# First head pair of block-sparse attention loaded in fp32 by hardware queues, mask rows spread by DMA, late transposes moved to the DMA crossbar

## The chip, the cores and the metric

The kernel runs on one core of one Trainium2 chip. The metric is device time in microseconds (us), from the median of a few executions. The kernel before takes 288.36 us (three runs, 288.26 to 288.44). TensorE is called PE in the profile, VectorE DVE, ScalarE ACT, GpSimd POOL and SyncE SP.

## The reference, cut to what matters

Attention with a block mask (band, global rows and columns, three sampled blocks for each block row), then an MLP-Mixer on its output: token mixing, residual, channel mixing, residual.

```python
# q, k, v: (4, 8, 768, 64) fp32; mask blocks of 32; 24 x 3 sampled blocks, int64
scores = scale * np.matmul(q, k.transpose(0, 1, 3, 2))
scores = np.where(mask, scores, -1000000000.0)
attn = np.exp(scores - scores.max(-1, keepdims=True)); attn = attn / (attn.sum(-1, keepdims=True) + 1e-09)
x = np.matmul(attn, v)             # regrouped to (4, 768, 512)
h = np.maximum(x.transpose(0, 2, 1) @ w_tok1, 0.0) @ w_tok2     # 768 -> 256 -> 768
u = x + h.transpose(0, 2, 1)
out = u + np.maximum(u @ w_ch1, 0.0) @ w_ch2                    # 512 -> 1536 -> 512
```

## The kernel before

The 32 heads are taken in 16 pairs. A pair has 12 steps: two query halves of 384 by six key chunks of 128. Each step is a pair of score matmuls (QK, one for each head), one exponential of 128x768 on ScalarE, and six matmuls with V (PV). The mask costs no instruction in a step. K and Q get 24 more rows each: on K's side a pattern that says which key belongs to which block, on Q's side 0 or -30000 for each block. The QK matmul then contracts over 88 rows instead of 64.

A small planner in the Python program simulates the engines with fixed costs and decides from that the order in which each engine gets its instructions. A changed cost or dependency can therefore move instructions far away. On TensorE the planner fills free time during attention with token and channel matmuls of batches that are through.

```python
# loads: cast from fp32 to bf16 on POOL's software queue, pair by pair
nc.gpsimd.dma_start(out=raw[:, :, :, :], in_=APx(src, 2 * p * S * D, ...))        # L230
# mask on 24 partitions R, after the sample has landed
nc.vector.tensor_copy(out=sampf[R, :], in_=samp64[R, :].bitcast(I32))
for dst, col in ((allow, 0), (eq0, 2), (eq1, 4)):
    nc.vector.tensor_scalar(..., op0=ALU.is_equal)
for other in (eq0, eq1, bandg):
    nc.vector.tensor_tensor(..., op=ALU.max)
nc.vector.tensor_scalar(out=t2add[R, :], ..., op0=ALU.mult, op1=ALU.add)
# mask rows: a matmul, two ScalarE copies, then 15 VectorE copies for eight head buffers
nc.vector.tensor_copy(out=bufs[n][R, :], in_=indf if nm == "k" else qtb[0][R, :])  # L356
# each pair: relayout on VectorE, 6 + 6 TensorE transposes, 4 evacuations (VectorE or ScalarE)
nc.vector.tensor_copy(out=buf[0:64, :], in_=i)                                     # L439
# ... step: QK (L470), exponential (L478), PV (L520)
# ... u: 24 TensorE transposes per batch (L628), first channel matmul L664, second L686
```

The softmax here doesn't subtract the row's maximum and nothing guards it: scores larger than these inputs give would overflow.

## Time and profile before

| what | before |
|---|---|
| span of the profiled run | 287.1 us |
| first QK matmul starts | 10.92 us |
| first exponential starts | 12.03 us |
| 25th exponential starts | 34.99 us |
| last exponential ends | 160.91 us |
| last QK matmul ends | 159.98 us |
| from there to the last matmul's end | 123.1 us |
| from there to the end of the span | 4.1 us |

These are boundaries between stages, and they add up to the span: attention ends with the last QK, and the tail is the PE work that is left then. The timelines give the first five, the windows the last three. The lines themselves stand in the prediction below.

Two rows of the chain of waits of the kernel before are added here, because the prediction did not look at them. Columns: start, duration, what.

```profile
13.73 0.64 PE ps L470 x2
14.38 0.33 PE po L520 x6
```

Two QK matmuls take 0.64 us here and six PV matmuls 0.33 us. The prediction works with 0.163 us for one QK and 0.030 us for one PV, the pace of later stages, which would make 0.33 and 0.18. TensorE runs at half of its later pace at this point. The first four exponentials take 16.88 - 12.03 = 4.85 us there instead of 4 x 0.750 = 3.0, so 1.85 of the 2.6 us of waits that the prediction puts down to VectorE fell before the stretch of the chain that it read, which starts at 16.9.

### The profile page before, as it was taken

The page shows a single profiled execution, that of the slowest core. Times are in us where ns is not written, and L with a number is a line of the kernel's source. Part 1 is how long each engine was busy: PE and PEld are TensorE (multiplying, and loading weights), DVE is VectorE, ACT ScalarE, POOL GpSimd, SP SyncE. Part 2 cuts the span into 40 slices and gives each one's busy share as a digit, 9 for nine tenths or more (in the row PEclk, how much of TensorE's full clock was granted, in tenths as well). Part 3 has the DMA queues.
Part 4 walks back from the last instruction along what each step waited for, and adds up shares of the span by engine and source line. Part 5 has one row for each costly group of instructions (what it writes and reads, how often), then busy time and mean ns, then how long its engine had stood idle before and what let it go on. Part 6 is the DMA issues. An engine that isn't in the chain of part 4 may idle for free.

```text
span 287.1 us, 6351 instructions
## 1 busy us (share of the span) xinstructions
PE 269.9 (94%) x2682; PEld 175.5 (61%) x2690; DVE 130.2 (45%) x286; ACT 191.9 (67%) x286; POOL 45.0 (16%) x70
## 2 busy tenths in 40 slices
PE   0799899999999999999999999999999999999994
PEld 0366676678777777777777754456544654456441
DVE  5789966557777569765546341210022001200121
ACT  1589999999999999999999642037501770067200
POOL 7956554522211000000000000000000000000000
PEclk9999999999999999999999999999999999999999
DMA  4999999996254100000000001220022001210122
GB/s 55 134 204 202 214 201 205 201 185 87 39 73 66 23 2 2 0 2 3 2 0 2 2 0 39 106 76 0 2 110 84 29 0 73 94 54 0 38 102 82
DMA packets 19168, 20.07 MB, mean 70 GB/s; under 512 B 1348, under 2 KB 15428, under 8 KB 19140
## 3 DMA queue, kind: packets, MB, share of 16 engines
q0 software_dynamic: 15648, 13.37, 30.3%
q1 hardware_dynamic: 3492, 6.29, 5.8%
q8 instruction: 21, 0.34, 0.5%
q14 instruction: 7, 0.06, 0.1%
HBM read 26.74 MB, written 6.29 MB: 115 GB/s over the span
## 4 chain that ended last, share of the span: by engine, by line
PE 73%; ACT 14%; DVE 6%; issue 2%; DMA 2%; POOL 2%; POOLq 0%; DVEq 0%; ACTq 0%
PE pm_ch L686 22%; PE pm_ch L664 21%; ACT et L478 14%; PE ps L470 14%; PE po L520 8%; PE pm_tok L578 3%; PE pm_tok L603 2%; DMA kraw<-in_k_dram 2%; DVE qtb L439 1%; PE pm_ut L628 1%; PE tq L421 1%; DVE ktb L439 1%; PE tk L421 1%; DVE x L535 1%; DVE klay L394 1%
## 5 line engine op out<-in xcount | busy, mean ns | idle before, releaser
L478 ACT ACTIVATE et<-ps 128x768 bf16<-128x768 f32 x192 | 143.2, 810 | 4.2 <-PE ps L470 3.2
L470 PE MATMUL ps<-qtb,ktb 88*128 88x384 bf16 x384 | 95.3, 329 | 4.0 <-ACT et L478 1.7
L560 ACT ACTIVATE rc<-pm_ch 128x384 bf16<-128x384 f32 x84 | 41.2, 491 | 60.7 <-PE pm_ch L664 44.8
L520 PEld LDWEIGHTS <-et 128*128 128x128 bf16 x1152 | 56.0, 97 | 22.8 <-DVE x L535 1.9
L664 PE MATMUL pm_ch<-uT,w_ch 128*128 128x384 bf16 x384 | 68.6, 326 | 0.2 <-DVE rc L562 0.2
L686 PE MATMUL pm_ch<-w_ch,rc 128*128 128x512 bf16 x280 | 62.4, 379 | 0.4
L520 PE MATMUL po<-vaug,et 128*128 128x65 bf16 x1152 | 61.5, 193 | 0.5 <-ACT et L478 0.2
L694 DVE TENSOR_TENSOR o<-pm_ch,x 128x512 f32<-128x512 f32 x24 | 16.6, 692 | 98.7 <-PE pm_ch L686 98.7
L664 PEld LDWEIGHTS <-w_ch 128*128 128x128 bf16 x384 | 37.0, 98 | 23.1 <-issue 0.3
L686 PEld LDWEIGHTS <-rc 128*128 128x128 bf16 x288 | 28.2, 98 | 33.6
L470 PEld LDWEIGHTS <-ktb 88*128 88x128 bf16 x384 | 34.2, 99 | 11.9 <-issue 4.4
L439 DVE COPY ktb<-tk 64x768 bf16<-64x768 bf16 x29 | 16.0, 552 | 17.5 <-PE tk L421 17.2
L611 DVE TENSOR_TENSOR x<-pm_tok,x 128x512 bf16<-128x512 f32 x24 | 16.2, 687 | 6.8 <-PE pm_tok L603 6.5
L535 DVE TENSOR_TENSOR x<-po,recip 128x384 bf16<-128x384 f32 x32 | 17.8, 557 | 1.1
L439 DVE COPY qtb<-tq 64x768 bf16<-64x768 bf16 x30 | 16.6, 552 | 2.1 <-PE tq L421 1.1
L603 PE MATMUL pm_tok<-a_t,w_tok 128*128 128x256 bf16 x96 | 17.0, 272 | 0.0
L230 POOL DMA_DIRECT2D vraw<-in_v_dram x16 | 12.3, 766 | 28.4 <-DVE vaug L391 25.7
L578 PE MATMUL pm_tok<-x,w_tok 128*128 128x256 bf16 x96 | 16.3, 272 | 0.0
L230 POOL DMA_DIRECT2D kraw<-in_k_dram x16 | 11.6, 727 | 7.7 <-DVE recip L534 2.2
L230 POOL DMA_DIRECT2D qraw<-in_q_dram x16 | 11.5, 720 | 6.4 <-DMA w_ch<-in_moe_w_ch_dram 2.4
L534 DVE RECIPROCAL recip<-po 128x6 f32<-128x6 f32 x32 | 6.2, 195 | 12.0 <-PE po L520 11.6
L421 PE MATMUL tq<-ident,qlay 128*128 128x128 bf16 x96 | 11.3, 230 | 0.2 <-DVE qlay L394 0.2
(49 smaller groups left out, 122.8 us busy)
## 6 DMA issues: line engine op xcount, KB each, us to landing
out_dram<-o SPq DMA_DIRECT2D x24, 256.0 KB, 2.0
kraw<-in_k_dram POOLq DMA_DIRECT2D x16, 192.0 KB, 7.9
qraw<-in_q_dram POOLq DMA_DIRECT2D x16, 192.0 KB, 7.4
vraw<-in_v_dram POOLq DMA_DIRECT2D x16, 192.0 KB, 7.0
w_ch<-in_moe_w_ch_dram POOLq DMA_DIRECT2D x8, 384.0 KB, 9.8
w_tok<-in_moe_w_tok_dram POOLq DMA_DIRECT2D x1, 384.0 KB, 7.8
w_tok2r<-in_moe_w_tok_dram POOLq DMA_DIRECT2D x1, 384.0 KB, 9.0
samp<-in_sampled_blocks_dram SPq DMA_DIRECT2D x1, 0.6 KB
```

The source lines that it names most:

```text
L230: nc.gpsimd.dma_start(out=raw[:, :, :, :], in_=APx(src, 2 * p * S * D, [[NC * D, 128], [S * D, 2], [1, NC * D]]),)
L421: nc.tensor.matmul(out=box["t"][:, c, :], lhsT=lays[nm][:, c, :, :].rearrange("p h d -> p (h d)"), rhs=ident[:, :], start=(c == 0), stop=( ...
L439: nc.vector.tensor_copy(out=buf[0:64, :], in_=i)
L470: nc.tensor.matmul(out=ps[:, hd, 0:384], lhsT=ktb[n][0:88, 128 * j : 128 * j + 128], rhs=qtb[n][0:88, 384 * half : 384 * half + 384], star ...
L478: nc.scalar.activation(out=et[:, :, :], in_=ps[:, :, 0:384], func=AF.Exp, scale=0.125)
L520: nc.tensor.matmul(out=po[:, hd, c, :], lhsT=et[:, hd, 128 * c : 128 * c + 128], rhs=va[:, hd, j, 0:65], start=(j == 0 and hd == 0 and c = ...
L535: nc.vector.tensor_tensor(out=free(xs[b][:, 3 * half, 128 * pb : 128 * pb + 128], 0, [[64, 2], [DM, 3], [1, 64]]), in0=po[:, :, :, 0:64], ...
L560: nc.scalar.activation(out=o(), in_=i, func=AF.Relu)
L578: nc.tensor.matmul(out=box["pm"][:, t, :], lhsT=w_tok1[:, sc, 128 * t : 128 * t + 128], rhs=xs[b][:, sc, 256 * g : 256 * g + 256], start=( ...
L603: nc.tensor.matmul(out=ubox["pm"][:, i, :], lhsT=w_tok2[:, t, 2 * s2 + i, :], rhs=a_t[:, t, :], start=(i == 0 and t == 0), stop=(i == 1 an ...
L664: nc.tensor.matmul(out=pbox["pm"][:, 0:384], lhsT=w_ch1[:, dmc, 128 * cc : 128 * cc + 128], rhs=st[b]["uT"][:, dmc, 384 * sh : 384 * sh + ...
L686: nc.tensor.matmul(out=pbox["pm"][:, :], lhsT=box["rc"][:, cc, 128 * sc : 128 * sc + 128], rhs=w_ch2[:, cc, :], start=(cc == 0), stop=(cc ...
```

## The change

The intent is to start attention earlier, to take copies off VectorE and ScalarE in the first pairs, and to free TensorE of transposes so that more channel matmuls fit into attention.

- K and Q of pair 0 are loaded as fp32 by the hardware queues of SyncE and ScalarE, and laid out, transposed and evacuated in halves of 384 positions, shared between the two engines.
- The mask chain after the sample's landing has five VectorE steps instead of eight. SyncE's DMAs spread the mask rows, for two heads at once, instead of 15 VectorE copies.
- For pairs 10 to 15 K and Q are laid out with their mask rows in a wide buffer, and a transposing DMA ("crossbar") writes the final layout: 12 transfers. The same is done for u of batches 1 to 3: six transfers.

```diff
+    NPE = 10
+    NL = 2
...
+    first(nc.sync, "k", k)
+    first(nc.scalar, "q", q)
     nc.sync.dma_start(out=samp64[R, :], in_=sampled_blocks)
-    load_pair(0, 1.5 * US, ("k", "q"))
...
-    for dst, col in ((allow, 0), (eq0, 2), (eq1, 4)):
-        nc.vector.tensor_scalar(
...
-    for other in (eq0, eq1, bandg):
-        nc.vector.tensor_tensor(out=allow[R, :], in0=allow[R, :], in1=other[R, :], op=ALU.max)
+    for col, other in ((0, bandg), (2, allow), (4, allow)):
+        nc.vector.scalar_tensor_tensor(
+            out=allow[R, :], in0=kbf[R, :], scalar=sampf[R, col : col + 1], in1=other[R, :],
+            op0=ALU.is_equal, op1=ALU.max,
...
+    for n in range(NV):
+        nc.sync.dma_start(out=ktb[n][R, :, :], in_=bandrows)
...
+    e2a = e2_mm(0, psM, "pm")
+    first_lay(vcopy, "k", 1)
+    kt0 = first_turn("k", 0)
+    qt0 = first_turn("q", 0)
+    e2_copy(vcopy, 0, 1, e2a)
+    e2_copy(acopy, 0, 0, e2a)
+    first_evac(vcopy, "k", 0, 0, kt0)
+    first_evac(acopy, "q", 0, 0, qt0)
...
-                def copy(eng, n=n, nm=nm, bufs=bufs):
-                    nc.vector.tensor_copy(
-                        out=bufs[n][R, :], in_=indf if nm == "k" else qtb[0][R, :]
-                    )
+            def spread(eng, n=n):
+                nc.sync.dma_start(out=qtb[n][R, :, :], in_=qtb[0][R, :, :])
...
+                nc.sync.dma_start_transpose(
+                    out=bufs[p % NV][:, :, :].rearrange("e h (c s) -> e (h c) s", c=NC),
+                    in_=wide[nm, p % NL][:, :, :, :].rearrange("p h c e -> p (h c e)"),
+                )
...
+        if b > 0:
+            turn_by_crossbar(b, g, u_evs)
+            return
```

## The prediction

> **What bounds the kernel now.** I read the page first (slices, then the chain), then the timelines of the start and of ScalarE, then the windows by stage.
>
> The slices show three stages: a start without matmuls, attention with both TensorE (PE) and ScalarE (ACT) full, and from about 160 us a tail in which ACT is mostly free and PE stays full.
>
> ```profile
> PE   0799899999999999999999999999999999999994
> DVE  5789966557777569765546341210022001200121
> ACT  1589999999999999999999642037501770067200
> ```
>
> The timeline of ACT says what attention costs: one exponential for each of 192 steps (16 head pairs of 12), starting at 12.03 us, ending at 149.57 + 11.34 = 160.91.
>
> ```profile
> 12.03 1.51 ACT L478 ACTIVATE et<-ps 128x768 bf16<-128x768 f32 x2 [1.16 <-PE ps L470]
> ...
> 16.88 15.16 ACT L478 ACTIVATE et<-ps 128x768 bf16<-128x768 f32 x20 [0.16 <-PE ps L470]
> 31.96 1.61 ACT L437 COPY ktb<-tk 64x768 bf16<-64x768 bf16 x2
> 33.91 0.80 ACT L437 COPY qtb<-tq 64x768 bf16<-64x768 bf16 x1 [0.33 <-DVE qtb L439]
> 34.99 25.27 ACT L478 ACTIVATE et<-ps 128x768 bf16<-128x768 f32 x34 [0.29 <-PE ps L470]
> ...
> 149.57 11.34 ACT L478 ACTIVATE et<-ps 128x768 bf16<-128x768 f32 x15
> ```
>
> The lines before 34.99 hold 24 exponentials, so 168 run from 34.99 to 160.91: 125.92 / 168 = 0.750 us each, with no idle worth naming. The first 24 took 22.96 us where 24 x 0.750 would be 18.0. The start of attention loses 5.0 us: 2.4 to the three copies above and 2.6 to waits. The chain of waits names the reason; from 16.9 to 32.6 us it runs almost wholly through VectorE (DVE), mask copies (L356) and evacuations of transposes (L439) among it.
>
> ```profile
> 18.16 0.45 DVE qtb L356
> 18.65 0.36 DVE vaug L391
> 19.04 0.35 DVE ktb L356
> ...
> 20.95 0.56 DVE ktb L439
> 21.52 0.55 DVE qtb L439
> 22.08 0.56 DVE qtb L439
> 22.64 1.12 DVE w_tok L705
> ```
>
> Last, the windows (PE first, then weight loads, DVE, ACT, POOL; the second number is the length):
>
> ```profile
> 99.26:159.98 60.72, 60.47 (x849) 46.32 (x849) 38.35 (x82) 60.42 (x82) 0.00 (x0) 1.00 0.01 2
> 159.98:283.06 123.08, 122.11 (x680) 65.17 (x684) 20.69 (x32) 43.56 (x88) 0.00 (x0) 1.00 0.13 50
> ```
>
> So the end is: the last QK matmul (159.98), plus 123.1 us of PE work left then, plus 4.1 us for the last add and store (287.14 - 283.06). The measured 288.36 is 1.3 above the span of 287.1.
>
> **What the Trainium skill says.** Four places.
> (1) "Perfetto Trace Analysis", Identifying the Most-Contended Engine: matmul busy time is a bad metric because matmuls are pipelined. This trace agrees: a channel matmul shows 326 ns, but the chain has 96 in 15.60 us, 0.1625 each. I therefore count PE by pace, all from the chain: QK 0.163, PV 0.030 (12 in 0.36), transpose 0.056 (7 in 0.39), token mixing 0.109 (4 in 0.44), second channel matmul 0.216 (72 in 15.54).
> (2) "VectorE: DVE Perf Modes", The three transpose paths: a 128x128 bf16 transpose takes 390 ns on TensorE and 1309 ns by the DMA crossbar. The trace has only the first, and at 0.056 us in a stream it is far cheaper than stated.
> (3) "Advanced Engine Details and Errata", X-Bar Transpose: transposing DMAs are about as fast as plain ones, 350 to 400 GB/s, and only one stream may transpose at a time. No run here shows it yet. The built program issues all 18 crossbar transfers from SyncE, so it keeps the rule.
> (4) "DMA: Bandwidth & Descriptors", Issuing engines are not separate DMA queues: two issuing engines share the same 16 DMA engines. The two hardware queues of the change thus save issue time and the software queue's delay, not bandwidth; the trace, whose loads all sit on one queue, does not test it.
>
> **The change, part by part.**
>
> *PE work.* In the built order the transposes into K and Q fall from 192 to 120 (pairs 10 to 15 go to the crossbar), those of u from 96 to 24 (batches 1 to 3), and 12 tiny mask matmuls come in: -144 x 0.056 + 12 x 0.03 = -7.7 us. This sits in attention, which ACT bounds, so it does not shorten attention itself. It is worth something only if other work moves in, and the order shows that it does: first-channel matmuls ahead of the last QK rise from 39 to 87. After the last QK, before has 345 + 288 channel matmuls, 24 token, 18 PV and 12 transposes: 345 x 0.1625 + 288 x 0.216 + 24 x 0.109 + 18 x 0.030 + 12 x 0.056 = 122 us (123.1 measured, so 1.1 of waits). The same count after, with 297 first-channel matmuls and no transposes, is 113.5; with the 1.1 it is **114.6**. The tail shrinks by 8.5 us.
>
> *First exponential.* Before: K and Q of pair 0 are cast on the software queue; the mask chain ends at 7.03, K is laid out at 7.05, then come transposes, a 0.80 us copy each, and the first QK pair is complete only after 11.46, when the last evacuation ends. After: POOL is free of two issues (0.83 + 0.72 us) ahead of its mask selects; the DVE mask chain has 5 steps instead of 8 once the sample has landed (seven at 0.17 to 0.82 plus the cast become the cast, three fused ones that I estimate at 0.5 and the last at 0.17: about 1.8 instead of 2.6 us); the work is in halves, split between DVE and ACT. Loads: 2 x 384 KB written instead of 2 x 192. From the 200 GB/s that this trace sustains on casting loads (where twice that is read) I estimate landing at 4.5 to 5.5 us; the sample stands behind K on its queue. Then 1.8 for the mask (7.0), 0.5 for its matmul, half transposes behind it, and two half evacuations of about 0.4 on each of two engines, with a copy of mask rows: first QK near 9, first exponential near **9.5**. That is 2.5 earlier.
>
> *Early DVE load.* Before makes 15 copies of mask rows at 0.37 us (5.5 us on DVE); after, seven DMAs do this. No K/Q evacuation in the ACT order falls to ACT after the first pair (three did, 2.4 us). Of the 5.0 us lost I keep 1.0 (a wait for V or for pair 1's loads): saves **4.0**.
>
> *DVE later.* It saves evacuations (24 K/Q halves and 6 of u at 0.55, 16 us), pays about 3.5 us for filling the wide buffers, and has about 22 relus in attention instead of 9. It was busy 38.35 of 60.72; it does not become the bound.
>
> *Sum.* 9.5 + 192 x 0.750 + 1.0 = 154.5 for the last exponential; the last QK is 0.9 earlier, 153.6; + 114.6 = 268.2; + 4.1 = 272.3 span; + 1.3 = 273.6. I add 0.4 for the tighter fit named below: **274.0 us**, 14.4 less.
>
> **Rivals.**
> (a) *The crossbar becomes the wait.* 16 of its 18 transfers must be through by about 140 us, and the first cannot start before some 65 to 70, when the wide buffers are filled: some 4.5 us each. At 384 KB and 350 GB/s (the page's figure) I estimate 1.1 us plus a fixed cost near the 2.0 that the stores in this trace show for 256 KB, so about 3. If 12 blocks cost 1.3 us one after the other, it is 15.7 us each, QK of the late pairs waits, and 16 x 15.7 = 251 us from 70 puts the kernel well beyond 400. Against it: the transfers stand three pairs ahead of need, and nothing else loads then (2 GB/s in the window above). At 5 to 6 us each it would cost 8 to 25 us.
> (b) *PE becomes the bound in attention.* By my pace, pairs 8 to 16 now hold 9.0 us of PE work each, against 12 x 0.750 = 9.0 of ACT. Before it was 8.2 to 9.1. With no slack, jitter can add 1 to 2%, up to 2 us: 276.
> (c) *The start gains nothing*, because fp32 loads land late or the rows spread by DMA arrive late: first exponential at 11.5 to 12, result 276 to 277.
> (d) *The early loss goes fully and the start is better than thought*: 271.
> (e) *All hidden*: attention is ACT-bound, so removing PE work saves nothing. The counted tail speaks against it: 8.5 us are removed after the last QK, where only PE runs.
>
> **Range and chances.** (b) and (c) add up to about 5 above, (d) takes 3 below: 270.5 to 278.5. For "within 2%" the time would have to stay above 282.6, which needs two of them together with a mild form of (a): 0.05. Slower needs the full form of (a): 0.02. Faster: 0.93.
>
> **What would show it.** First exponential near 9.5; the 24th ends by 29 instead of 34.99; no ACT copies between exponentials; last QK near 153 to 154; the window from there to the last matmul 114 to 115; PE with 132 fewer matmuls; crossbar transfers landing in about 3 us, none of them as releaser of a QK matmul. A QK that waits for a DMA at 95 us or later would prove (a); ACT idle of 0.05 or more per step in the late pairs would prove (b); a first exponential after 11 would prove (c). The prediction is wrong if the tail does not shrink by 8 us, or if attention does not end 5 us earlier.

## The result

The changed kernel takes 276.25 us (four runs, 276.14 to 276.51) beside 288.37 us for the kernel before (288.26 to 288.44). The ratio is 0.9581, with a 95% interval of 0.9565 to 0.9598. A ratio here and below is the mean time of one kernel's fast runs over that of the other's of the same rounds, so it is not quite the ratio of the medians quoted. The gain is 12.1 us where 14.4 were predicted; the time lies inside the range. The prediction calls 34.99 the end of the 24th exponential; it is where the 25th starts, behind three copies, and the tables say so.

| what | before | predicted | after |
|---|---|---|---|
| first QK | 10.92 | about 9 | 9.54 |
| first exponential | 12.03 | 9.5 | 10.56 |
| 25th exponential starts | 34.99 | by 29 | 31.03 |
| last exponential ends | 160.91 | 154.5 | 157.80 |
| last QK ends | 159.98 | 153.6 | 156.87 |
| from there to the last matmul's end | 123.1 | 114.6 | 113.65 |
| from there to the end of the span | 4.1 | 4.1 | 3.9 |

The slices of the kernel after:

```profile
PE   0899999999999999999999999999999999999994
DVE  2748988766965464653625442300221003300122
ACT  2679999999999999999999920077104750077100
```

PE is as full as before and the three stages are still there. VectorE is less loaded in the first half.

The ScalarE timeline of the kernel after (start, length, engine, line, operation, out<-in, count, and in brackets the idle time and what ended it):

```profile
10.56 1.51 ACT L610 ACTIVATE et<-ps 128x768 bf16<-128x768 f32 x2 [0.15 <-PE ps L601]
12.69 1.51 ACT L610 ACTIVATE et<-ps 128x768 bf16<-128x768 f32 x2 [0.62 <-PE ps L601]
14.38 0.81 ACT L610 ACTIVATE et<-ps 128x768 bf16<-128x768 f32 x1 [0.18 <-PE ps L601]
16.02 0.81 ACT L610 ACTIVATE et<-ps 128x768 bf16<-128x768 f32 x1 [0.82 <-PE ps L601]
17.30 0.81 ACT L610 ACTIVATE et<-ps 128x768 bf16<-128x768 f32 x1 [0.48 <-PE ps L601]
18.34 69.72 ACT L610 ACTIVATE et<-ps 128x768 bf16<-128x768 f32 x93 [0.22 <-PE ps L601]
88.31 69.49 ACT L610 ACTIVATE et<-ps 128x768 bf16<-128x768 f32 x92 [0.25 <-PE ps L601]
```

No copy stands between exponentials any more. From 18.34 on, 185 exponentials run to 157.80: (157.80 - 18.34) / 185 = 0.754 us each, almost without a gap. Everything that is lost is lost before: seven exponentials take 18.34 - 10.56 = 7.78 us where 7 x 0.750 = 5.25 would do, so 2.5 us. Each of the gaps is ended by TensorE's QK.

The chain of waits of the kernel after says how TensorE spent this time:

```profile
7.94 0.57 DVE qtb L373
8.53 0.48 ACT qtb L373
9.05 0.48 PE tkfirst L351 x3
9.54 0.48 PE ps L601
...
16.31 0.32 PE tk L555 x3
16.63 0.64 PE ps L601 x2
...
17.97 0.34 PE ps L601 x2
```

Two QK still take 0.64 us at 16.63 and only 0.34 at 17.97. Three transposes take 0.32 (0.107 each) at 16.31; in the prediction's count a transpose costs 0.056. The Trainium skill, "TensorE: Matmul & The Clock Gate", section "Part 1: The HAM clock gate", describes this: the array runs at half its clock until it has been busy for about 3.4 us, with about 107 ns for a 128-column matmul at half and 56 ns at full clock. The two durations agree with the trace. The 3.4 us do not come out so simply: from the first QK at 9.54 on TensorE is busy for 7.84 of 8.13 us before the pace doubles at 17.67. The first two lines show another wait, to which experiment e8_two_banks comes back.

The two late windows of the kernel after (columns as in the prediction):

```profile
96.15:156.87 60.72, 60.72 (x797) 44.39 (x796) 29.95 (x66) 60.49 (x81) 0.00 (x0) 1.00 0.44 70
156.87:270.52 113.65, 113.61 (x628) 59.88 (x624) 19.10 (x29) 37.85 (x77) 0.00 (x0) 1.00 0.18 61
```

The stretch after the last QK is 9.4 us shorter than before (123.08 to 113.65), and PE is busy in all of it.

Where a crossbar transfer appears in the chain, it looks like this:

```profile
78.08 7.61 DMA qtb<-qwide
...
85.77 0.36 DVE qwide L492
```

Q of pair 10 takes 7.6 us from the start of its issue to landing. Of that the issue itself holds SyncE for 3.00 us, and K of the same pair was issued on the same queue 2.95 us before, so 7.6 us is an upper bound for the transfer alone. The next instruction in the chain is no QK but a VectorE copy that refills the wide buffer, and so must wait until the transfer has read it. VectorE waits 2.0 us for that, and the exponentials lose the 0.25 us shown at 88.31.

### The profile page after: what moved, and what is told of

The parts are those of the page before. It is cut to its first block, busy times and chain, and to the rows that moved or that the text cites. A ratio compares the mean times of both kernels' runs of the same rounds, so it can differ in the third digit from the quotient of the medians.

```text
span 274.4 us, 6116 instructions
## 1 busy us (share of the span) xinstructions
PE 260.7 (95%) x2558; PEld 167.6 (61%) x2558; DVE 116.4 (42%) x260; ACT 184.5 (67%) x273; POOL 44.0 (16%) x68
## 4 chain that ended last, share of the span: by engine, by line
PE 81%; ACT 9%; DMA 4%; DVE 3%; issue 1%; SPq 0%; ACTq 0%; DVEq 0%
PE pm_ch L847 23%; PE pm_ch L824 22%; PE ps L601 18%; PE po L654 10%; ACT et L610 9%; PE pm_tok L757 3%; PE pm_tok L732 3%; DMA qtb<-qwide 3%; DMA samp<-in_sampled_blocks_dram 1%; PE tk L555 1%; PE pm_ut L786 0%; DVE x L669 0%; DVE ktb L570 0%; PE tq L555 0%; DVE klay_first L343 0%
## 5 line engine op out<-in xcount | busy, mean ns | idle before, releaser
L696 ACT ACTIVATE rc<-pm_ch 128x384 bf16<-128x384 f32 x74 | 36.3, 491 | 59.3 <-PE pm_ch L824 43.3
L824 PE MATMUL pm_ch<-uT,w_ch 128*128 128x384 bf16 x384 | 72.1, 326 | 0.0
L847 PE MATMUL pm_ch<-w_ch,rc 128*128 128x512 bf16 x288 | 63.3, 379 | 0.0
L824 PEld LDWEIGHTS <-w_ch 128*128 128x128 bf16 x384 | 36.2, 98 | 20.9
L601 PEld LDWEIGHTS <-ktb 88*128 88x128 bf16 x384 | 35.0, 99 | 12.0 <-issue 4.3
L698 DVE TENSOR_SCALAR rc<-pm_ch 128x384 bf16<-128x384 f32 x22 | 12.2, 552 | 12.2 <-PE pm_ch L824 12.1
L570 DVE COPY ktb<-tk 64x768 bf16<-64x768 bf16 x18 | 9.9, 552 | 8.4 <-PE tk L555 8.2
L570 DVE COPY qtb<-tq 64x768 bf16<-64x768 bf16 x18 | 10.0, 553 | 1.1 <-PE tq L555 0.7
```

The source lines that it names most:

```text
L570: nc.vector.tensor_copy(out=buf[0:64, hd, :], in_=i)
L601: nc.tensor.matmul(out=ps[:, hd, 0:384], lhsT=ktb[n][0:88, hd, 128 * j : 128 * j + 128], rhs=qtb[n][0:88, hd, 384 * half : 384 * half + 38 ...
L696: nc.scalar.activation(out=o(), in_=i, func=AF.Relu)
L824: nc.tensor.matmul(out=pbox["pm"][:, 0:384], lhsT=w_ch1[:, dmc, 128 * cc : 128 * cc + 128], rhs=st[b]["uT"][:, dmc // 2, 3 * sh : 3 * sh + ...
L847: nc.tensor.matmul(out=pbox["pm"][:, :], lhsT=box["rc"][:, cc, 128 * sc : 128 * sc + 128], rhs=w_ch2[:, cc, :], start=(cc == 0), stop=(cc ...
```

## The experiments

There were twelve runs, among them one repeat of the changed kernel. All gave correct outputs. Edits are against the changed kernel. Gains between experiments are the difference of two ratios times 288.4 us, unless a trace is named.

### e1_start_only, e7_u_pe: splitting the gain

e1_start_only undoes the crossbar (it keeps the new start), e7_u_pe undoes only its part for u.

```diff
# e1_start_only
-    NPE = 10
+    NPE = 16
-        if b > 0:
+        if b > 3:
-    P.stream(-1, wide_stream())
# e7_u_pe
-        if b > 0:
+        if b > 3:
```

> The changed kernel with every crossbar transpose undone (all K, Q and u transposes on TensorE again), the new start kept. Theory of the prediction: the counted tensor work after the last QK goes back from 113.5 to 122.6 us, attention itself keeps its length, so the time is 276.25 + 8 to 9 = 284 to 285.5 us, and the new start is worth 3 to 4 us by itself. Rival: the crossbar part is worth little because its transfers (7.6 us to landing, with a 2 us wait on VectorE) give it back; then this run is within 3 us of 276.

> The changed kernel with only the transposes of u back on TensorE (K and Q of pairs 10 to 15 stay on the crossbar). By count the tensor work after the last QK goes from 113.5 to 117.4 us, so 276.25 + 3.9 = about 280.2 us. If the crossbar transfers of K and Q cost something that those of u do not (the 2 us wait of VectorE at 84 us), the split is not half and half: the whole crossbar part was worth 9 us (285.2 against 276.25).

e1_start_only took 285.64 us, ratio 0.989 (0.9865 to 0.9916). Its profiled run fell in the slow state (granted clock, the share of its full clock that TensorE got, 0.765; 355.67 us) and its trace is not used; the three fast runs are 284.63 to 285.75. e7_u_pe took 280.51 us, ratio 0.9722 (0.9706 to 0.9738).

So the new start is worth (1 - 0.989) x 288.4 = 3.2 us, the crossbar for u (0.9722 - 0.9581) x 288.4 = 4.1, and that for K and Q (0.989 - 0.9722) x 288.4 = 4.8, since the two runs differ by it alone. The parts are priced one on top of the other, the start first, then K and Q, then u; the interval of e1_start_only leaves the first two open by 0.7 us each way. In e7_u_pe the last exponential ends at 157.88, as in the changed kernel (157.80), but 118.1 us of tail follow instead of 113.6. The part for u thus works in the tail alone.

### e4_rows_dve: who writes the mask rows

The mask rows of pairs 1 to 3 go back to twelve VectorE copies.

```diff
-    for n in range(NV):
-        nc.sync.dma_start(out=ktb[n][R, :, :], in_=bandrows)
+    nc.sync.dma_start(out=ktb[0][R, :, :], in_=bandrows)
...
-                nc.sync.dma_start(out=qtb[n][R, :, :], in_=qtb[0][R, :, :])
+    # for each head and for ktb and qtb:
+                        nc.vector.tensor_copy(
+                            out=bufs[n][R, hd, :], in_=indf if bufs is ktb else qtb[0][R, hd, :]
+                        )
```

> The changed kernel with the mask rows of pairs 1 to 3 copied by VectorE again (12 copies of about 0.35 us) instead of six DMAs. Theory of the prediction (VectorE was what held the first exponentials back): about 4 us of VectorE work comes back in the first 35 us and costs 1 to 3 us, 277 to 279. Rival (the first exponentials are held by the tensor array at half rate, VectorE has room): within 0.5 us of 276.25.

It took 282.93 us, ratio 0.9808 (0.9786 to 0.983). That is 6.5 us above the changed kernel, far more than either theory said. The ScalarE timeline of e4_rows_dve shows how:

```profile
28.79 0.79 ACT L573 COPY ktb<-tk 64x768 bf16<-64x768 bf16 x1
29.48 0.79 ACT L573 COPY qtb<-tq 64x768 bf16<-64x768 bf16 x1
32.44 0.79 ACT L573 COPY ktb<-tk 64x768 bf16<-64x768 bf16 x1 [2.17 <-PE tk L560]
34.77 1.51 ACT L615 ACTIVATE et<-ps 128x768 bf16<-128x768 f32 x2 [1.54 <-PE ps L606]
```

With VectorE later, the planner gave three evacuations to ScalarE (2.4 us), and ScalarE then waited 2.17 + 1.54 us plus 0.62 further on. During these waits TensorE had little to do and fell back to half pace: in the chain of this run four QK take 1.28 us at 34.04. The 24th exponential ends at 38.42 instead of 31.10. Copies and gaps are about 6.6 of these 7.3 us; the array also doubled its pace 1.8 us later than in the changed kernel, at 19.48. How much each of the three (order, copies, pace) would cost alone was not separated. Nor is 6.5 us the price of the copies: the kernel before makes 15 such copies, and its 25th exponential starts at 34.99, while here it starts at 38.35. The run shows what copies cost that upset the build order.

### e2_warm, e5_warm_hold: the slow array at the start

Both add matmuls that nothing reads, into a PSUM tile that is free then, to bring TensorE to its full pace earlier. e2_warm puts 16 at the very start and four short ones behind the first transposes. e5_warm_hold spreads fillers up to the third QK pair.

```diff
# both; warm(n, cols) issues n matmuls into an unread tile
+    warm(16, 390)
# e2_warm
     qt0 = first_turn("q", 0)
+    warm(4, 128)
# e5_warm_hold
     e2a = e2_mm(0, psM, "pm")
+    warm(2, 390)
     qt0 = first_turn("q", 0)
+    warm(6, 390)
     # and warm(1, 390) behind the second K transposes, the 2nd and the 3rd QK pair
```

> The changed kernel with 16 matmuls of 390 columns on a constant tile from about 1.6 us, and 4 of 128 columns behind the first Q transposes, whose result nobody reads. Theory A (the early loss is a tensor array at half rate until 17.7 us): full rate is reached before 9 us, QK matmuls pace at 0.163 instead of 0.320 from the start, the first exponential moves from 10.56 to about 10, the first 24 exponentials take 18.5 to 19.5 us instead of 20.5, and the time falls by 1.5 to 2.5 us to about 274.2. Theory B (the early loss is order of work and late data): nothing moves, 276.2 or a little more.

> The changed kernel with the 16 unread matmuls of the warm run, and further ones wherever TensorE would stand idle until the third QK pair: 2 behind the mask product, 6 behind the first Q transposes, 1 behind the second K transposes, 1 behind each of the second and third QK pairs (390 columns each). In the warm run full rate came at 5.9 us and was lost again before 9.5 us, after a stretch in which TensorE was busy less than half of the time. Theory A (the array keeps full rate only while it is kept busy, and half rate is what the early exponentials wait for): QK paces at 0.163 from the first one, the first 24 exponentials take 18.5 to 19.5 us instead of 20.5, the time falls by 1 to 2 us to 274.3 to 275.3. Theory B (order and data): no change in the first 24 exponentials, 276.3 or a little more.

e2_warm took 275.86 us, ratio 0.9557 (0.9531 to 0.9582), an interval that overlaps the changed kernel's. The PE timeline of e2_warm:

```profile
9.04 0.33 PE L363 MATMUL tkfirst<-ident,klay_first 128*128 128x128 bf16 x3 [0.81 <-ACT qtb L385]
9.54 1.62 PE L614 MATMUL ps<-qtb,ktb 88*128 88x384 bf16 x4 [0.17 <-ACT qtb L371]
```

Three transposes at 9.04 are fast (0.33 against 0.48 in the changed kernel), but the four QK at 9.54 take 1.62 us, exactly what they take in the changed kernel. The array had come up at 5.9 us and fell back by 9.54, although no two matmuls in between started more than 1.03 us apart. The windows of e2_warm, whose column behind POOL is the granted clock, show the fall:

```profile
5.89:9.31 3.42, 1.98 (x18) 1.09 (x17) 3.19 (x10) 0.77 (x2) 3.42 (x5) 1.00 1.11 163
9.31:19.55 10.24, 9.79 (x70) 5.99 (x69) 5.31 (x18) 7.26 (x11) 6.39 (x10) 0.50 1.19 212
```

TensorE had 1.98 us of work in the 3.42 us before the fall, and then stayed at half for 10.24 us although it was nearly always busy. The run failed to do what it was made for, so it decides nothing about the theory.

e5_warm_hold took 274.20 us (273.52 to 274.29), ratio 0.9498 (0.9481 to 0.9516). Its ScalarE timeline:

```profile
10.42 12.71 ACT L628 ACTIVATE et<-ps 128x768 bf16<-128x768 f32 x17
24.37 131.66 ACT L628 ACTIVATE et<-ps 128x768 bf16<-128x768 f32 x175 [1.24 <-PE ps L617]
```

Seventeen exponentials run without a gap from the first on, 0.748 us each: the 2.5 us are gone. The PE timeline of e5_warm_hold shows the pace. Three QK take 0.65 us from 10.04 on, where the chain of the changed kernel has 1.12:

```profile
10.04 0.65 PE L617 MATMUL ps<-qtb,ktb 88*128 88x384 bf16 x3 [0.18 <-DVE ktb L371]
```

The run has more matmuls than the changed kernel, not fewer, so it was the pace of the array that cost them. About half is given back at once. The chain of waits of e5_warm_hold names the gap of 1.24 us:

```profile
9.95 11.21 DMA w_tok2r<-in_moe_w_tok_dram
21.19 1.19 DVE w_tok L886
```

A token weight, whose load took 11.2 us, lands at 21.17. VectorE had been given its 1.19 us copy ahead of the evacuations of K and Q for pair 2, and those are late by that wait. In the changed kernel this wait was hidden behind the slow array.

### e3_samp_first, e8_two_banks: an earlier first exponential

The chain of the changed kernel begins with the sample's load (4.05 us to landing, behind K on the same queue), and has VectorE and ScalarE copy mask rows from one PSUM tile one after the other (7.94 and 8.53, shown above). e3_samp_first issues the sample ahead of K. e8_two_banks makes the mask product twice, into two banks, one for each engine.

```diff
# e3_samp_first
+    nc.sync.dma_start(out=samp64[R, :], in_=sampled_blocks)
     first(nc.sync, "k", k)
     first(nc.scalar, "q", q)
-    nc.sync.dma_start(out=samp64[R, :], in_=sampled_blocks)
# e8_two_banks
+    e2b = e2_mm2()                      # the same product in a tile of the QK pool
-    e2_copy(acopy, 0, 0, e2a)
+    e2_copy(acopy, 0, 0, e2b)
```

> The changed kernel with the load of the sampled blocks issued ahead of K on the same queue. Theory A (the mask chain waits for a sample that stands behind K, 4.05 us, and holds the layout of K on VectorE): the sample is there by 3.2 us, the mask is done near 4.7 instead of 6.86, the layout of K starts near 5.5, the first exponential near 9.2 instead of 10.56, and the time falls by about 1.3 us to 275. Theory B (K itself lands no earlier than 6.9, or the half rate of the tensor array only lasts longer after an earlier start): under 0.5 us.

> The changed kernel with the first mask product made twice, into two banks of PSUM, so that the VectorE copy and the ScalarE copy of it read different banks. Theory A (the two engines took turns because both read one bank: 7.94 to 8.50 on VectorE, then 8.53 to 9.00 on ScalarE): the ScalarE copy starts near 8.0, the Q evacuations near 8.5, the first exponential moves from 10.56 to 10.1, the time falls by 0.3 to 0.5 us. Theory B (ScalarE waits for something else, the Q transposes): no change.

e3_samp_first took 275.49 us, ratio 0.954 (0.9513 to 0.9567): 1.2 us better than the changed kernel, with intervals that just touch. Its profiled run was slow (clock 0.858), so only the time is used. e8_two_banks took 275.1 us, ratio 0.9552 (0.9516 to 0.9589). The interval overlaps that of the changed kernel, so its worth in time is not settled. The ScalarE timeline of e8_two_banks settles the wait itself:

```profile
7.75 0.47 ACT L380 CAST qtb<-ps_e 24x384 bf16<-24x384 f32 x1 [1.95 <-PE ps_e L374]
...
10.04 1.51 ACT L618 ACTIVATE et<-ps 128x768 bf16<-128x768 f32 x2 [0.15 <-PE ps L609]
```

ScalarE's copy starts at 7.75 instead of 8.53, now next to VectorE's, and the first exponential at 10.04 instead of 10.56. The Trainium skill, "PSUM — Partial Sum Buffer", section "Terms", says that two engines on the same bank and quadrant at once raise an error. The built kernel keeps them apart, and here that order cost 0.5 us. Since the run gives the second reader a tile of its own as well as a bank of its own, it does not tell whether the order in the built kernel comes from the bank or from the tile.

### e6_all_start, e9_tok2_later, e10_rows_early, e12_tok2_and_fill: putting it together

e6_all_start joins the early sample, fillers (9, 3, 3, 1, 1) and the two banks. e9_tok2_later adds a later slot for the token weight's copy, e10_rows_early moreover builds the key pattern ahead of the band on POOL. e12_tok2_and_fill is e9_tok2_later with a still later slot. I chose that slot because in its built order 87 first-channel matmuls stand ahead of the last QK again, as in the changed kernel; in e9_tok2_later there were 75.

```diff
# e9_tok2_later: Ev(24 * US); e12_tok2_and_fill: Ev(28 * US); both on e6_all_start
-    tok2_op = P.op(("dve",), {"dve": 900.0}, [tok2_raw], wtok2_lay, prio=3)
+    tok2_op = P.op(("dve",), {"dve": 900.0}, [tok2_raw, Ev(28 * US)], wtok2_lay, prio=3)
# e10_rows_early, on e9_tok2_later: the two selects of ind stand ahead of the four of bandg,
# and bandg is joined to the mask by a last max
```

> The start with all that was found: the sample loaded ahead of K, the first mask product made twice in two banks so that VectorE and ScalarE need not take turns on one, and unread matmuls that keep TensorE busy until the third QK pair. If the causes add up (sample 1.2, turns on one bank 0.5, half rate 1 to 2): first exponential near 8.6, the 24th done by 27.5 instead of 31.1, time 272.8 to 274. If the half rate comes back in spite of the filling: about 274.5 to 275.

> The kernel with all start changes, and the one VectorE copy that waited 2.5 us for a token-mixing weight (17.79 to 20.29 us) put later in the order by the planner. Theory A (the earlier start was given back there: ScalarE then stood idle 2.24 us before 24.24): that idle time goes, the last exponential ends 1.5 to 2.2 us earlier, 272.2 to 273 us. Theory B (another load is as late, or ScalarE catches up anyway): within 0.5 us of the run before it.

> As the run before, with the block indicator made by GpSimd ahead of the band, so that the DMA of the mask rows of K is issued at about 3.1 instead of 4.35 us, for one short VectorE instruction more. Theory A (with the other causes gone the first QK waits for that DMA, 1.33 us, until 8.75): the rows land near 7.5, the first exponential comes at 8.0 to 8.4 instead of 9.27, the time falls by another 0.8 us to 271.5 to 272.2. Theory B (the rows land when the K and V loads ahead of them are through, not by their issue): no change.

> As the run with the later token-mixing copy, with that copy still some 4 us later in the plan. The built order then again has 87 first-channel matmuls ahead of the last QK, as the changed kernel has, where that run had 75. Theory A (that run brought the last exponential forward to 154.6 us and gave 2 us back because 12 channel matmuls, 12 x 0.1625 = 1.95 us, had moved behind it): the last exponential stays near 154.6 and the work after the last QK goes from 116.0 back to 113.9 us, span near 271.2, time near 272.9 us. Theory B (attention is itself limited by TensorE): the last exponential moves back to about 156 and the span stays near 273.

e6_all_start: 275.0 us (273.67 to 277.05), ratio 0.9537 (0.9487 to 0.9587), no better than e5_warm_hold. Its ScalarE timeline:

```profile
9.27 12.73 ACT L636 ACTIVATE et<-ps 128x768 bf16<-128x768 f32 x17 [1.26 <-PE ps L625]
24.24 0.81 ACT L636 ACTIVATE et<-ps 128x768 bf16<-128x768 f32 x1 [2.24 <-PE ps L625]
```

Its first exponential is 1.15 us ahead of e5_warm_hold's and the gap behind the 17th is 1.0 us longer. The token weight does land 0.9 us earlier (20.27), but behind that wait the array falls to half pace from 22.17 to 25.58 (granted clock 0.50): two QK take 0.64 us at 23.50. The last exponential ends at 156.03 in both. So the expectation's second branch came true, the half rate that comes back. It did not come back in every execution: the one with a mean granted clock of 1.000 took 273.67 us, the others 274.30, 275.70 and 277.05 with 0.991, 0.993 and 0.986.

e9_tok2_later: 274.92 us, ratio 0.9551 (0.9521 to 0.9581). The last exponential came at 154.62, 1.4 us earlier, but the tail was 115.6 us long instead of 113.6: twelve channel matmuls fewer lay in attention, 12 x 0.1625 = 1.95 us. e10_rows_early: 275.13 us, ratio 0.9549 (0.9531 to 0.9567); the first exponential came at 9.74 instead of the 8 or so hoped for, because the band was now the late part and the array was slow until 10.92 in that run, where the fillers themselves, at half pace, stood in the chain for 2.4 us ahead of the first QK.

e12_tok2_and_fill: 273.44 us (273.28 to 274.54), ratio 0.9477 (0.9464 to 0.949). The tail is back at 113.6. Its profiled run is the slowest of its five (span 272.8, the others 271.6 to 271.8), and its ScalarE timeline still has a gap:

```profile
9.12 14.96 ACT L636 ACTIVATE et<-ps 128x768 bf16<-128x768 f32 x20 [1.11 <-PE ps L625]
25.70 0.81 ACT L636 ACTIVATE et<-ps 128x768 bf16<-128x768 f32 x1 [1.63 <-PE ps L625]
```

Now it is V of pair 2 that lands late (issued 13.10, 10.8 us), and the array falls to half pace behind that gap, from 25.09 to 28.50. This is nevertheless the lowest ratio: 0.9477 / 0.9581 = 0.989, so about 1.1% below the changed kernel and 5.2% below the one before. Its interval overlaps that of e5_warm_hold, so it is not shown that the later steps gained anything over the fillers alone.

### c_after_again: the changed kernel once more

> The changed kernel once more, as the control of these runs on one chip: 276.25 us as before, within 0.3%, ratio to the kernel before 0.958.

It took 276.42 us, ratio 0.9579 (0.9566 to 0.9592), the same as before. In this trace the array came to full pace at 19.15 us instead of 17.67, with the same program, and the 24th exponential ended at 31.70 instead of 31.10. So the point at which the pace doubles is not fixed by the program. In both traces it doubles at the end of the first stretch of 3.41 us in which TensorE shows 3.41 us of work; the stretch before that, cut at the same step, shows 3.16 us in both. That this is the condition is not shown: in e12_tok2_and_fill the pace doubled after a stretch with 2.95 us of work.

## Why the prediction was right or wrong

The predicted sum against the measured one, term by term:

| term | predicted | measured | miss |
|---|---|---|---|
| first exponential | 9.5 | 10.56 | +1.1 |
| 192 exponentials at 0.750, and what is lost | 144.0 + 1.0 | 144.0 + 3.2 | +2.2 |
| last QK before the last exponential's end | -0.9 | -0.9 | 0.0 |
| PE after the last QK | 114.6 | 113.65 | -0.95 |
| last add and store | 4.1 | 3.9 | -0.2 |
| time beyond the span | 1.3 + 0.4 | 1.85 | +0.15 |
| sum | 274.0 | 276.25 | +2.25 |

*PE work: right.* The count of 87 channel matmuls ahead of the last QK holds, and so does the count of matmuls: 2682 and 2558 are in the traces, of which before lacks eight channel records, so 132 fewer. The prediction's own sign, at least 8 us off the tail, came true: it fell by 9.4 us, and the 0.95 us beyond the predicted 8.5 are mostly the 1.1 us of waits that the prediction carried over: after has about 0.2. e9_tok2_later confirms the pricing from the other side: 12 channel matmuls fewer in attention made the tail 2 us longer. Rival (e), that all of it is hidden, is refuted by e7_u_pe.

*First exponential: mechanism right, size off by 1.1.* The mask is ready at 6.86 us, as the 7.0 of the prediction. Behind it, "two half evacuations of about 0.4 on each of two engines, with a copy of mask rows" was too short: the two mask copies take turns (0.5 us, e8_two_banks). The half pace of the array adds 0.14 (10.56 against 10.42 in e5_warm_hold). The rest, about 0.4, is that the first QK pair is not complete with the first Q evacuation. Its second matmul starts at 10.04, after the second evacuation.

*Early DVE load: partly right, and here is the step that failed.* The copies and their wait are gone as predicted. The first 24 exponentials with all that follows up to the 25th take 31.03 - 10.56 = 20.47 us instead of 22.96, which saves 2.5 us and not 4.0. The step "Of the 5.0 us lost I keep 1.0 (a wait for V or for pair 1's loads)" failed: 2.5 us stayed until 18.34, and neither load had a part in it. TensorE ran at half pace there, and one step of the first pairs needs more than 0.750 us then. For example two QK of 0.64, six PV of 0.33 and three transposes of 0.32 lie between 15.98 and 17.27 in the chain, for 1.29 us. The cause is shown by e5_warm_hold, which removes the loss with useless matmuls alone. The prediction took all paces from one steady stage and did not check them in the stage to which it applied them; the two lines of before shown above had it. A wait of the predicted kind did exist behind it, for the token weight and for V of pair 2, and came out as soon as the array was fast. The prediction called itself wrong if attention did not end 5 us earlier. The last exponential came 3.1 us earlier, so by that sign this part was wrong; e1_start_only prices the new start at the same 3.2 us.

*The steady part.* After 18.34 the exponentials lose 0.004 us each, 0.7 us in all. Rival (b), PE as the bound in attention, would have shown 0.05 a step and is refuted in that form. With the 2.5 before, this is the 3.2 of the table.

*Time beyond the span: a slip that did no harm.* The prediction set the median of 288.36 against the span of the profiled execution, which itself took 288.84: 1.7 us beyond its span, as in the changed kernel (276.14 and 274.4). The 0.4 us added for another reason, the tighter fit, made up for it by luck.

*Crossbar: right in effect, wrong in size.* The estimate was 3 us for a transfer, and the one seen in the chain landed after 7.6, issue included. It stayed harmless because transfers stand three pairs ahead of need: rival (a) shows up as VectorE's 2.0 us wait for a wide buffer and 0.25 us of ScalarE.

*Rivals (c) and (d).* The first exponential was 1.5 us earlier than before, so (c) is refuted as it stands, though part of the gain it doubted was indeed missing. (d), 271 us, was not reached even with the start mended by hand: e12_tok2_and_fill reaches 273.44.

What stays open: why e4_rows_dve costs 6.5 us cannot be divided among its three parts, the traces give no landing time for most crossbar transfers, and the slow state of single runs on this one-core program (clock 0.765 and 0.858) is not explained.

## What to carry to other kernels

Take the pace of an operation from the stage that the argument is about: a start with few matmuls can run at half the pace that the same instructions have later, and a few unread matmuls kept up through the first steps bought 2 us here. A gain at the start is kept only if the next late arrival moves too, so look for the loads that land just after the gap before counting it. Matmul time that is freed in a stage with another bound becomes worth something exactly when the built order shows other work moving into it.

## What the Trainium skill lacked or had wrong

- "TensorE: Matmul & The Clock Gate", section "Why this matters for your kernels", asks that no idle gap be over about 3 us, or the array falls back to half clock. In e2_warm it fell back at 9.31 us although no two matmuls since 5.9 had started more than 1.03 us apart. TensorE shows 1.98, 2.02, 2.00 and 2.02 us of work in the 3.4 us before the falls in e2_warm, e6_all_start, e4_rows_dve and e12_tok2_and_fill; in e9_tok2_later 2.22 us, from 5.40 to 8.81, did not end in a fall. Once fallen, it stayed at half for 3.41 (e6, e12), 6.82 (e4) or 10.24 us (e2), in e2_warm with TensorE busy for 9.79 of 10.24. The free-running window of about 3.4 us that Part 1 describes fits these lengths.
- The same page, Part 1, warns that clock records may be unreliable; no page says what a profile's granted clock shows before its first record. In the changed kernel the record starts at 17.67, where the pace doubles, and the window 10.56 to 18.34 has 1.00 in that column while two QK take 0.64 us instead of 0.33. A later fall does show: 0.50 from 9.31 to 19.55 in e2_warm.
- "VectorE: DVE Perf Modes", section "The three transpose paths", gives 390 ns for TensorE and 1309 ns for the crossbar for one 128x128 block. In a stream the trace has 56 ns on TensorE at full pace and 107 ns at half. Twelve blocks of Q of pair 10 landed 7.6 us after the start of their issue, 0.63 us a block at most.
- "Advanced Engine Details and Errata", section "X-Bar Transpose", says transposing DMAs are as fast as plain ones, at 350 to 400 GB/s. That transfer wrote 384 KB in 7.6 us from the start of its issue to landing, about 52 GB/s at the least, while plain stores of 256 KB took 2.0 us in the kernel before. The issue alone held SyncE's sequencer for 1.4 to 3.1 us, for which this page has no figure.
- "PSUM — Partial Sum Buffer" has the rule that two engines must not be on one bank and quadrant, but no price for keeping it: taking turns on one tile in one bank cost 0.5 us of the first exponential here (10.56 against 10.04).
